# A recurrent-memory attention step on one core: one product for a maximum, one for each mask, a 64-wide turn of the memory, and a projection unit split in two

## The chip, the cores and the metric

The kernel runs on one core of one Trainium2 chip. The metric is the device time of one execution in microseconds (us). "Engine" below means one of the core's instruction streams: PE multiplies matrices (PEld is its weight loading, which overlaps it), DVE and ACT work on vectors, POOL is the general-purpose one, SP issues transfers.

## The reference

Four layers follow each other, A, B, A, B, each added to a residual of 2048 tokens by 640 channels. The change is in layer B, cut here to what matters:

```python
for s in range(n_seg):                       # 64 segments of 32 tokens
    xs = x[:, s * 32:(s + 1) * 32, :]
    h = concatenate([mem, xs], axis=1)       # 8 memory rows + 32 tokens = 40 rows
    q, k, v = h @ Wq, h @ Wk, h @ Wv         # 32 heads of 128, each from 640 channels
    scores = q @ k.T * scale                 # 40 x 40 for each head
    scores = where(mask, scores, -1e9)
    p = softmax(scores)
    o = (p @ v) @ Wo                         # back to 640 channels
    mem = o[:, :8, :]                        # memory of the next segment
    outs.append(o[:, 8:, :])
```

Segment s + 1 needs the memory that segment s made, so the 64 segments of a layer run one after the other, in two layers: 128 steps.

## The kernel before, in words

`layer_B` holds one loop over the 64 steps. The instructions of PE, ACT, DVE and POOL run in exactly the order in which the code issues them (`_OrdNC` chains each engine's instructions), so the order of the lines is the order on each engine.

The 32 tokens and 8 memory rows of a step are held so that 32 rows (24 tokens and the memory, `b_HX`) go through the step itself, and the other 8 tokens of each segment (the "tail" rows) go through projections for four steps at a time (`b_TX`). Most products have a stationary operand of only 32 columns. Four of them are placed side by side in PE's array, at columns 0, 32, 64 and 96 (`tile_position=(0, 32 * j)`), and run at the same time. The profile writes such a product's weights as 128*32. The products of probabilities with values use 32 (or 8) rows and all 128 columns instead (32*128, 8*128), and the turns of normalised tokens use the whole array (128*128).

One step goes as follows. The names are those of the tiles in the profile.

1. K and Q of heads 0 to 15, then of heads 16 to 31 (`b_Ka`, `b_Qa`, `b_Kb`, and Q's second half as `b_Qb` and `b_Qc`), each five groups of four products. ACT copies each out of PSUM and DVE transposes it (`turn`) into `b_KT` and `b_QT`.
2. For each half of the heads, a (b = 0) and b (b = 1): `mask_mm` writes the mask into a PSUM tile `b_SP` by products of an identity with `b_mask5`, and `scores` adds 32 small products per half. Groups of V of half a (`b_Va`) stand between them.
3. The softmax of each half: `soft_max` (DVE, negated maximum), `soft_sub` (DVE adds it to the scores), `soft_exp` (ACT), `soft_sum` and `soft_rec` (DVE), `soft_p` (POOL multiplies), `p_turn` (two DVE transposes into `b_PTa` or `b_PTb`).
4. Meanwhile PE does V of half b (`b_Vb`, five groups), one chunk of a deferred output projection (`od_chunk(0)`, tile `b_OPSd`), one tail unit (`tail_unit`, tile `b_tail`: five groups that project the tail rows of a later group of four steps), and in some steps `ln_spread` (five whole-array turns, `b_lntps`; 15 blocks of 128 tokens and 3 blocks of tail rows per layer are spread inside the loop). ACT copies the tail unit out (`b_tu`).
5. `pv(0)` and `pv(1)`: probabilities times values of the halves (`b_OTP`), copied by DVE and ACT into `b_OTsb`. DVE turns the tail unit (`tail_turn`).
6. Two groups of a small unit of V of tail rows (`b_vtail`, five groups in all), the output projection (`b_OPS`, 64 products), `od_chunk(1)`, a `b_vtail` group. In one step of four, and three more per layer, DVE begins a layer norm here (`ln_begin`).
7. The memory: ACT copies `b_OPS` in three parts into `b_msb`; for each part PE turns it by small products with `b_sel` (`b_MT`), followed by a group of `b_vtail` after the first and second part, and DVE copies the result into the next step's `b_HX`. The next `b_Ka` waits for that.

The PSUM tiles of steps 1 to 7 come in rotation from five buffers, and `b_tail` (shared with `b_Qc`), the tile of `b_OPS` (shared with `b_lntps`) and `b_OPSd` have one each.

Of the kernel before, what the change touches and what calls it, by code (L numbers as in the profile page):

```python
# [18 lines left out]
F32 = mybir.dt.float32  # L19
BF16 = mybir.dt.bfloat16  # L20
ACT = mybir.ActivationFunctionType
ALU = mybir.AluOpType
AX = mybir.AxisListType
# [6 lines left out]
NCH = 5  # L30
# [776 lines left out]
def layer_B(nc, tc, C, W, x_src, xb_src, x_dst, mem0, B_Wv, B_Wo, nsteps=64, out_bf16=False, tag=""):  # L807
    SCB = 1.0 / math.sqrt(128.0)
    nc_raw = nc
    nc = _OrdNC(tc, nc_raw, engines=ORDER_ENGINES)  # L810
# [3 lines left out]
    with ExitStack() as ctx:  # L814
# [16 lines left out]
        wkl = pool("b_wkl", 1)  # L831
        wk = pool("b_wk", 1)
        sm = pool("b_sm", 2)
# [5 lines left out]
        po = psum("b_po", 1)  # L839

        def ps_tile(shape, dtype, name):
            return pp.tile(shape, dtype, name=name, tag="ps")
# [3 lines left out]
        mask5, selm = C.mask5, C.selm  # L846
# [14 lines left out]
        def evac(eng, dst, src, scale=None):  # L861
            if eng == "act":
                if scale is None:
                    nc.scalar.copy(dst, src)
                else:
                    nc.scalar.activation(out=dst, in_=src, func=ACT.Copy, scale=scale)
            else:
                if scale is None:
                    nc.vector.tensor_copy(dst, src)
                else:  # L870
                    nc.vector.tensor_scalar(out=dst, in0=src, scalar1=scale, scalar2=None, op0=ALU.mult)
# [40 lines left out]
        def cols_of(u):  # L912
            return HX[u // 4][:, :, u % 4, :]

        def thin_mm(cols_ap, Wt, b, name, c0=0, c1=NCH, ps=None):
            if ps is None:
                ps = ps_tile([128, 512], F32, name)
            for c in range(c0, c1):
                for j in range(4):
                    n = 4 * b + j  # L920
                    nc.tensor.matmul(ps[32 * j:32 * j + 32, :], lhsT=cols_ap[:, c, :], rhs=Wt[:, c, 512 * n:512 * n + 512],
                                     start=(c == 0), stop=(c == NCH - 1), tile_position=(0, 32 * j), skip_group_check=True)
            return ps

        def by_head(cols_ap, Wt, h0, nh, ps):
            for c in range(NCH):
                wt = Wt[:, c, 128 * h0:128 * (h0 + nh)].rearrange("p (h e) -> p h e", e=128)
                for j in range(4):
                    nc.tensor.matmul(ps[32 * j:32 * j + 32, :].rearrange("p (h x) -> p h x", x=32), lhsT=cols_ap[:, c, :], rhs=wt[:, :, 32 * j:32 * j + 32],
                                     start=(c == 0), stop=(c == NCH - 1), tile_position=(0, 32 * j), skip_group_check=True)  # L930
            return ps
# [16 lines left out]
        def tail_cols(g, c=None):  # L948
            v = TX[g // 4][:, :, 4 * (g % 4):4 * (g % 4) + 4, :].rearrange("p c s t -> p c (s t)")
            return v if c is None else v[:, c]  # L950

        def tail_unit(g, k, ps):
            proj, b = divmod(k, 2)
            return by_head(tail_cols(g), W.wq if proj else W.wk, 16 * b, 16, ps)

        def tail_evac(k, ps):
            sb = kqp.tile([128, 512], BF16, name="b_tu", tag="kq")
            evac("act", sb[:], ps[:], SCB if k // 2 else None)
            return sb
# [47 lines left out]
        for k in WO_FIRST + WO_LAST:  # L1007
            f = load_B_wo(nc, W, B_Wo, k)
# [7 lines left out]
        tsb = []  # L1016
        for k in range(4):
            ps = tail_unit(0, k, ps_tile([128, 512], F32, "b_tail"))
# [13 lines left out]
        for k in range(4):  # L1032
            ps = vtail_unit(0, k)
# [56 lines left out]
        for s in range(nsteps):  # L1090
            last = (s == nsteps - 1)
            u = s + 1
            cols = cols_of(s)
            unit = (s // 4 + 1, s % 4) if s // 4 + 1 < NG else None
            work = unit or (None if last else (NG - 1, 0))
# [13 lines left out]

            def mask_mm(b):  # L1110
                SP = ps_tile([128, 5, 40], F32, f"b_SP{b}")
                for j in range(4):
                    nc.tensor.matmul(SP[32 * j:32 * j + 32].rearrange("p g k -> p (g k)"), lhsT=C.identb[:, 32 * j:32 * j + 32], rhs=mask5[:].rearrange("p g k -> p (g k)"),
                                     start=True, stop=False, tile_position=(0, 32 * j), skip_group_check=True)
                return SP

            def scores(b, SP):
# [6 lines left out]
                            nc.tensor.matmul(SP[32 * j:32 * j + 32, 0 if tail else 1 + i, :], lhsT=lhsT, rhs=KT[s][:, h, :],  # L1124
                                             start=False, stop=True, tile_position=(0, 32 * j), skip_group_check=True)

            negmax = sm.tile([128, 2, 5], F32, name="b_negmax", tag="negmax")
            ssum = sm.tile([128, 2, 5], F32, name="b_ssum", tag="ssum")
            rs = sm.tile([128, 2, 5], F32, name="b_rs", tag="rs")
            E_ = wk.tile([128, 2, 5, 40], BF16, name="b_E", tag="E0")  # L1130

            def soft_max(b, SP):
                nc.vector.tensor_reduce(out=negmax[:, b, :], in_=SP[:], axis=AX.X, op=ALU.max, negate=True)

            def soft_sub(b, SP):
                nc.vector.tensor_tensor(out=SP[:], in0=SP[:], in1=negmax[:, b, :].unsqueeze(2).to_broadcast([128, 5, 40]), op=ALU.add)

            def soft_exp(b, SP):
                nc.scalar.activation(out=E_[:, b], in_=SP[:], func=ACT.Exp)

            def soft_sum(b):
                nc.vector.tensor_reduce(out=ssum[:, b, :], in_=E_[:, b], axis=AX.X, op=ALU.add)

            def soft_rec(b):
                nc.vector.reciprocal(out=rs[:, b, :], in_=ssum[:, b, :])

            def soft_p(eng, b):
                eng.tensor_tensor(out=Pn[:, b, :, 0:40], in0=E_[:, b], in1=rs[:, b, :].unsqueeze(2).to_broadcast([128, 5, 40]), op=ALU.mult)

            def p_turn(b, PT):  # L1150
                nc.vector.transpose(out=PT[:, :, :, 8:40], in_=Pn[:, b, 1:5, :].rearrange("p g (a k) -> p a g k", a=2))
                nc.vector.transpose(out=PT[:, :, :, 0:8], in_=Pn[:, b, 0, :].rearrange("p (a i t) -> p a i t", a=2, i=4))
# [20 lines left out]
            for b in range(2):  # L1173
                for nm, Wt, D_, scale in (("K", W.wk, KT, None), ("Q", W.wq, QT, SCB)):
# [4 lines left out]
                    else:  # L1179
                        ps = by_head(cols, Wt, 16 * b, 16, ps_tile([128, 512], F32, f"b_{nm}{'ab'[b]}"))  # L1180
# [5 lines left out]
            SPb = mask_mm(1)  # L1186
            thin_mm(cols, W.wv, 0, "b_Va", 3, 4, Va)
            scores(1, SPb)
            thin_mm(cols, W.wv, 0, "b_Va", 4, NCH, Va)
            PTa = wkl.tile([128, 2, 4, 40], BF16, name="b_PTa", tag="PTa")  # L1190
            PTb = wkl.tile([128, 2, 4, 40], BF16, name="b_PTb", tag="PTb")
            soft_max(0, SPa)
            soft_sub(0, SPa)
            soft_exp(0, SPa)
            soft_max(1, SPb)
            soft_sub(1, SPb)
            soft_sum(0)
            soft_rec(0)
            soft_p(nc.gpsimd, 0)
            soft_exp(1, SPb)  # L1200
            evac("act", VH[s][:, 0, :], Va[:])
            soft_sum(1)
            soft_rec(1)
            soft_p(nc.gpsimd, 1)
            p_turn(0, PTa)
            p_turn(1, PTb)
            Vb = thin_mm(cols, W.wv, 1, "b_Vb")
            evac("act", VH[s][:, 1, :], Vb[:])
            if not last:
                od_chunk(0)  # L1210

            if work:
                tps = tail_unit(work[0], work[1], po.tile([128, 512], F32, name="b_tail", tag="tail"))
            if unit:
                tsb = tail_evac(unit[1], tps)
            if ln_ready:
                ln_spread(ln_ready.pop(0), po.tile([128, NCH, 4, 32], BF16, name="b_lntps", tag="ops"))
            if last:
# [9 lines left out]
            OTv = OTsb[:].rearrange("p (a x) -> p a x", a=2)  # L1228
            pv(0, PTa, ots)
            evac("dve", OTv[:, 0, 0:160], otf[0][:].rearrange("p i c -> p (i c)"))  # L1230
            ot01 = ps_tile([128, 4, 40], F32, "b_OTP1")
            ots[0][1] = ot01[:]
            pv(1, PTb, ots)
            evac("act", OTv[:, :, 160:320], otf[1][:].rearrange("p a i c -> p a (i c)"))
            evac("dve", OTv[:, 1, 0:160], ot01[:].rearrange("p i c -> p (i c)"))
            evac("act", OTv[:, :, 480:640], otf[3][:].rearrange("p a i c -> p a (i c)"))
            evac("dve", OTv[:, :, 320:480], otf[2][:].rearrange("p a i c -> p a (i c)"))
            if not last and (s + 1) % 4:
                vtails_in(s + 1)
# [17 lines left out]
            if not last:  # L1257
                dst = cols_of(s + 1)
                msb = wk.tile([128, 320], BF16, name="b_msb", tag="msb")
                parts = ((0, 1), (1, 3), (3, NCH))  # L1260
                for ca, cb in parts:
                    nc.scalar.copy(msb[:, 64 * ca:64 * cb], ops[:, 64 * ca:64 * cb])
                for pi, (ca, cb) in enumerate(parts):
                    mt = ps_tile([128, cb - ca, 8], F32, f"b_MT{pi}")
                    for c in range(ca, cb):
                        for q in range(4):
                            o = 64 * c + 32 * (q % 2)
                            nc.tensor.matmul(mt[32 * q:32 * q + 32, c - ca, :], lhsT=msb[:, o:o + 32], rhs=selm[:, q // 2, :],
                                             start=True, stop=True, tile_position=(0, 32 * q), skip_group_check=True)
                    nc.vector.tensor_copy(dst[:, ca:cb, 24:32], mt[:])  # L1270
                    vtail_some((1, 1, NCH)[pi])
            vtail_some(NCH)
# [114 lines left out]
```

## Time and profile before

| what | value |
|---|---|
| time, 3 runs | 2427.61, 2425.11, 2420.36 us; median 2425.11 |
| the profiled execution | 2418.85 us, its span 2417.1 us |
| granted clock of PE | 0.997 |
| PE busy | 2289.2 us (95%), 62330 products |
| DVE busy | 1882.4 us (78%) |
| ACT busy | 1416.2 us (59%) |
| POOL busy | 749.8 us (31%) |

The span runs from the first to the last instruction. The profiled execution's own time is 1.75 us more than its span. In the rows of the timeline the columns are: start in us from the span's start, duration in us (of all merged instructions together), engine, line, operation, what is written and read, count, and in brackets the idle time before it with what ended it. Most of layer B's rows have the line of one helper (L113), so they are told apart by tile.

### The profile page before, as it was taken

The numbers are of one execution on the slowest core, as the hardware profiler recorded it, in microseconds if no ns is written. First come the engines' busy times: TensorE is split into PE (matmuls) and PEld (weight loads), VectorE is DVE, ScalarE is ACT, GpSimd is POOL, SyncE is SP. The second block draws the span as 40 slices with busy tenths as digits, with TensorE's granted clock in tenths as the row PEclk, the third lists the DMA queues.
The fourth block names the chain that finished last, engine by engine and source line by source line (L and its number), as shares of the span: only waits on it lengthen the run. The fifth ranks groups of instructions, "written<-read, shape, count | busy, mean of one in ns | idle before, by whom it ended". The sixth has DMA issues, their size and how long they took to land.

```text
span 2417.1 us, 139330 instructions
## 1 busy us (share of the span) xinstructions
PE 2289.2 (95%) x62330; PEld 1504.1 (62%) x62330; DVE 1882.4 (78%) x4695; ACT 1416.2 (59%) x3198; POOL 749.8 (31%) x1589
## 2 busy tenths in 40 slices
PE   8999999999999999999989999999999999999998
PEld 5566656666666666666655665566666666666665
DVE  8999877777777777777679998777777777777776
ACT  6999964444444444444369999644444444445443
POOL 5677641111111111111146776411111111111111
PEclk9999999999999999999999999999999999999999
DMA  4121271111111111111220211711111111111110
GB/s 168 47 85 60 73 260 27 28 32 32 29 30 30 31 29 32 29 31 28 65 88 17 64 45 38 274 24 26 29 28 27 27 27 28 27 29 29 27 24 20
DMA packets 168883, 123.38 MB, mean 51 GB/s; under 512 B 104652, under 2 KB 153180, under 8 KB 166492
## 3 DMA queue, kind: packets, MB, share of 16 engines
q1 hardware_dynamic: 167288, 112.69, 16.4%
q8 instruction: 487, 7.98, 1.4%
q10 hardware_dynamic: 996, 1.79, 0.2%
q14 instruction: 112, 0.92, 0.1%
HBM read 79.60 MB, written 34.80 MB: 47 GB/s over the span
## 4 chain that ended last, share of the span: by engine, by line
PE 67%; DVE 14%; ACT 9%; DMA 4%; issue 3%; POOL 1%; SPq 1%; ACTq 0%; DVEq 0%; POOLq 0%
PE b_OPS L113 11%; PE b_Ka L113 6%; PE b_Kb L113 5%; PE b_Qa L113 5%; DVE a_nm L142 5%; PE b_tail L113 5%; PE b_Va L113 4%; PE b_Vb L113 4%; ACT a_PT L142 4%; PE b_vtail L113 4%; PE a_S L113 3%; PE b_SP L113 2%; PE b_OPSd L113 2%; PE b_OTP L113 2%; PE b_Qb L113 2%
## 5 line engine op out<-in xcount | busy, mean ns | idle before, releaser
L113 PEld LDWEIGHTS <-b_HX 128*32 128x32 bf16 x17920 | 467.0, 96 | 269.0 <-DVE b_HX L113 3.6
L113 POOL TENSOR_TENSOR b_Pn<-b_E,b_rs 128x200 bf16<-128x200 bf16 x256 | 133.4, 522 | 1092.7 <-DVE b_rs L113 1074.6
L142 DVE TENSOR_REDUCE a_nm<-a_S 128x2 f32<-128x512 f32 (+3 forms) x512 | 395.4, 817 | 52.8 <-PE a_S L113 37.5
L142 ACT ACTIVATE a_PT<-a_T 128x1024 bf16<-128x1024 f32 (+1 forms) x384 | 345.5, 905 | 22.8 <-PE a_T L113 15.0
L113 PE MATMUL b_OPS<-b_wo,b_OTsb 128*32 128x320 bf16 x8192 | 306.5, 300 | 4.6 <-DVE b_OTsb L113 3.6
L113 PEld LDWEIGHTS <-b_OTsb 128*32 128x32 bf16 x8192 | 208.1, 96 | 73.8 <-DVE b_OTsb L113 24.8
L113 DVE STREAM_TRANSPOSE b_KT<-b_kq 128x512 bf16<-128x512 bf16 x256 | 181.3, 708 | 80.3 <-ACT b_kq L113 79.7
L142 POOL TENSOR_SCALAR_AFFINE_SELECT a_PT<-a_PT 128x256 bf16<-128x256 bf16 x380 | 189.3, 503 | 152.5 <-ACT a_PT L142 151.0
L113 ACT ACTIVATE b_E<-b_SP 128x200 bf16<-128x200 f32 x256 | 86.3, 337 | 235.5 <-DVE b_SP L113 225.4
L113 PE MATMUL b_Va<-b_wv,b_HX 128*32 128x512 bf16 x2560 | 222.4, 381 | 0.0
L113 DVE CAST b_HX<-b_MT 128x16 bf16<-128x16 f32 (+1 forms) x380 | 64.7, 172 | 198.3 <-PE b_MT L113 190.0
L113 DVE STREAM_TRANSPOSE b_QT<-b_kq 128x256 bf16<-128x256 bf16 (+1 forms) x384 | 184.2, 505 | 39.3 <-ACT b_kq L113 35.9
L113 ACT CAST b_msb<-b_OPS 128x64 bf16<-128x64 f32 x378 | 69.3, 256 | 213.2 <-PE b_OPS L113 213.2
L113 PEld LDWEIGHTS <-b_TX 128*32 128x32 bf16 x5360 | 144.1, 96 | 58.4 <-issue 5.3
L113 DVE CAST b_OTsb<-b_OTP 128x160 bf16<-128x160 f32 (+1 forms) x384 | 133.8, 376 | 44.7 <-PE b_OTP L113 40.8
L113 PE MATMUL b_Ka<-b_wk,b_HX 128*32 128x512 bf16 x2560 | 163.5, 381 | 1.0 <-DVE b_HX L113 0.9
L113 PE MATMUL b_Vb<-b_wv,b_HX 128*32 128x512 bf16 x2560 | 162.2, 379 | 0.0
L113 PE MATMUL b_Qa<-b_wq,b_HX 128*32 128x512 bf16 x2560 | 161.1, 379 | 0.0
L113 PE MATMUL b_Kb<-b_wk,b_HX 128*32 128x512 bf16 x2560 | 161.1, 379 | 0.0
L113 PE MATMUL b_vtail<-b_wv,b_TX 128*32 128x256 bf16 x2680 | 149.7, 273 | 1.3 <-issue 0.7
L113 ACT CAST b_kq<-b_Ka 128x512 bf16<-128x512 f32 x128 | 74.9, 585 | 123.0 <-PE b_Ka L113 123.0
L113 ACT CAST b_OTsb<-b_OTP 128x320 bf16<-128x320 f32 x256 | 96.5, 429 | 81.4 <-PE b_OTP L113 81.0
(185 smaller groups left out, 5048.3 us busy)
## 6 DMA issues: line engine op xcount, KB each, us to landing
b_wv<-in_B_Wv_dram SPq DMA_DIRECT2D x10, 1024.0 KB
b_wo<-in_B_Wo_dram SPq DMA_DIRECT2D x16, 640.0 KB
b_VT<-b_VTd SPq DMA_DIRECT2D x504, 16.0 KB
b_XO<-xres SPq DMA_DIRECT2D x256, 30.0 KB
b_VTd<-b_vt SPq DMA_DIRECT2D x480, 16.0 KB
b_xt<-xres_bf SPq DMA_DIRECT2D x40, 160.0 KB
b_wk<-in_B_Wk_dram SPq DMA_DIRECT2D x20, 256.0 KB
b_wq<-in_B_Wq_dram SPq DMA_DIRECT2D x20, 256.0 KB
```

The lines of the kernel that those rows point to most:

```text
L113: r = f(*a, **k)
L142: r = f(*a, **k)
```

## The change

Five edits, all inside `layer_B`:

- The negated maximum of half b is made in BF16, and `soft_sub(1)` no longer is a DVE addition but one whole-array product of the identity with that maximum, repeated along the 40 columns, added to the scores in PSUM. It stands on PE after the third of the five groups of `b_Vb`; before the change all of `b_Vb` was issued in one piece. Half a keeps its DVE addition.
- Each mask is written by one whole-array product in place of four products of 32 columns.
- The memory is turned by products whose stationary operand is 64 columns wide: two for each 128 channels in place of four.
- The tail unit is split: three groups stand where it stood, two stand between `pv(0)` and `pv(1)`. Its copy by ACT (`b_tu`) moves behind both of ACT's copies into `b_OTsb`.
- Order of the softmax: `soft_exp(1)` is issued before `soft_sum(0)`; `p_turn(0)` ahead of POOL's second product.

```diff
--- before.py
+++ after.py
@@ -922,8 +922,8 @@
                                      start=(c == 0), stop=(c == NCH - 1), tile_position=(0, 32 * j), skip_group_check=True)
             return ps
 
-        def by_head(cols_ap, Wt, h0, nh, ps):
-            for c in range(NCH):
+        def by_head(cols_ap, Wt, h0, nh, ps, c0=0, c1=NCH):
+            for c in range(c0, c1):
                 wt = Wt[:, c, 128 * h0:128 * (h0 + nh)].rearrange("p (h e) -> p h e", e=128)
                 for j in range(4):
                     nc.tensor.matmul(ps[32 * j:32 * j + 32, :].rearrange("p (h x) -> p h x", x=32), lhsT=cols_ap[:, c, :], rhs=wt[:, :, 32 * j:32 * j + 32],
@@ -949,9 +949,9 @@
             v = TX[g // 4][:, :, 4 * (g % 4):4 * (g % 4) + 4, :].rearrange("p c s t -> p c (s t)")
             return v if c is None else v[:, c]
 
-        def tail_unit(g, k, ps):
+        def tail_unit(g, k, ps, c0=0, c1=NCH):
             proj, b = divmod(k, 2)
-            return by_head(tail_cols(g), W.wq if proj else W.wk, 16 * b, 16, ps)
+            return by_head(tail_cols(g), W.wq if proj else W.wk, 16 * b, 16, ps, c0, c1)
 
         def tail_evac(k, ps):
             sb = kqp.tile([128, 512], BF16, name="b_tu", tag="kq")
@@ -1109,9 +1109,8 @@
 
             def mask_mm(b):
                 SP = ps_tile([128, 5, 40], F32, f"b_SP{b}")
-                for j in range(4):
-                    nc.tensor.matmul(SP[32 * j:32 * j + 32].rearrange("p g k -> p (g k)"), lhsT=C.identb[:, 32 * j:32 * j + 32], rhs=mask5[:].rearrange("p g k -> p (g k)"),
-                                     start=True, stop=False, tile_position=(0, 32 * j), skip_group_check=True)
+                nc.tensor.matmul(SP[:].rearrange("p g k -> p (g k)"), lhsT=C.identb[:], rhs=mask5[:].rearrange("p g k -> p (g k)"),
+                                 start=True, stop=False, skip_group_check=True)
                 return SP
 
             def scores(b, SP):
@@ -1124,16 +1123,20 @@
                             nc.tensor.matmul(SP[32 * j:32 * j + 32, 0 if tail else 1 + i, :], lhsT=lhsT, rhs=KT[s][:, h, :],
                                              start=False, stop=True, tile_position=(0, 32 * j), skip_group_check=True)
 
-            negmax = sm.tile([128, 2, 5], F32, name="b_negmax", tag="negmax")
+            negmax = [sm.tile([128, 5], dt_, name=f"b_negmax{b}", tag=f"negmax{b}") for b, dt_ in enumerate((F32, BF16))]
             ssum = sm.tile([128, 2, 5], F32, name="b_ssum", tag="ssum")
             rs = sm.tile([128, 2, 5], F32, name="b_rs", tag="rs")
             E_ = wk.tile([128, 2, 5, 40], BF16, name="b_E", tag="E0")
 
             def soft_max(b, SP):
-                nc.vector.tensor_reduce(out=negmax[:, b, :], in_=SP[:], axis=AX.X, op=ALU.max, negate=True)
+                nc.vector.tensor_reduce(out=negmax[b][:], in_=SP[:], axis=AX.X, op=ALU.max, negate=True)
 
             def soft_sub(b, SP):
-                nc.vector.tensor_tensor(out=SP[:], in0=SP[:], in1=negmax[:, b, :].unsqueeze(2).to_broadcast([128, 5, 40]), op=ALU.add)
+                shift = negmax[b][:].unsqueeze(2).to_broadcast([128, 5, 40])
+                if b:
+                    nc.tensor.matmul(SP[:], lhsT=C.identb[:], rhs=shift, start=False, stop=True, skip_group_check=True)
+                else:
+                    nc.vector.tensor_tensor(out=SP[:], in0=SP[:], in1=shift, op=ALU.add)
 
             def soft_exp(b, SP):
                 nc.scalar.activation(out=E_[:, b], in_=SP[:], func=ACT.Exp)
@@ -1187,32 +1190,31 @@
             thin_mm(cols, W.wv, 0, "b_Va", 3, 4, Va)
             scores(1, SPb)
             thin_mm(cols, W.wv, 0, "b_Va", 4, NCH, Va)
-            PTa = wkl.tile([128, 2, 4, 40], BF16, name="b_PTa", tag="PTa")
-            PTb = wkl.tile([128, 2, 4, 40], BF16, name="b_PTb", tag="PTb")
             soft_max(0, SPa)
             soft_sub(0, SPa)
             soft_exp(0, SPa)
             soft_max(1, SPb)
+            Vb = thin_mm(cols, W.wv, 1, "b_Vb", 0, 3)
+            PTa = wkl.tile([128, 2, 4, 40], BF16, name="b_PTa", tag="PTa")
+            PTb = wkl.tile([128, 2, 4, 40], BF16, name="b_PTb", tag="PTb")
             soft_sub(1, SPb)
+            soft_exp(1, SPb)
+            thin_mm(cols, W.wv, 1, "b_Vb", 3, NCH, Vb)
             soft_sum(0)
             soft_rec(0)
             soft_p(nc.gpsimd, 0)
-            soft_exp(1, SPb)
             evac("act", VH[s][:, 0, :], Va[:])
             soft_sum(1)
             soft_rec(1)
+            p_turn(0, PTa)
             soft_p(nc.gpsimd, 1)
-            p_turn(0, PTa)
             p_turn(1, PTb)
-            Vb = thin_mm(cols, W.wv, 1, "b_Vb")
             evac("act", VH[s][:, 1, :], Vb[:])
             if not last:
                 od_chunk(0)
 
             if work:
-                tps = tail_unit(work[0], work[1], po.tile([128, 512], F32, name="b_tail", tag="tail"))
-            if unit:
-                tsb = tail_evac(unit[1], tps)
+                tps = tail_unit(work[0], work[1], po.tile([128, 512], F32, name="b_tail", tag="tail"), 0, 3)
             if ln_ready:
                 ln_spread(ln_ready.pop(0), po.tile([128, NCH, 4, 32], BF16, name="b_lntps", tag="ops"))
             if last:
@@ -1228,12 +1230,16 @@
             OTv = OTsb[:].rearrange("p (a x) -> p a x", a=2)
             pv(0, PTa, ots)
             evac("dve", OTv[:, 0, 0:160], otf[0][:].rearrange("p i c -> p (i c)"))
+            if work:
+                tail_unit(work[0], work[1], tps, 3, NCH)
             ot01 = ps_tile([128, 4, 40], F32, "b_OTP1")
             ots[0][1] = ot01[:]
             pv(1, PTb, ots)
             evac("act", OTv[:, :, 160:320], otf[1][:].rearrange("p a i c -> p a (i c)"))
             evac("dve", OTv[:, 1, 0:160], ot01[:].rearrange("p i c -> p (i c)"))
             evac("act", OTv[:, :, 480:640], otf[3][:].rearrange("p a i c -> p a (i c)"))
+            if unit:
+                tsb = tail_evac(unit[1], tps)
             evac("dve", OTv[:, :, 320:480], otf[2][:].rearrange("p a i c -> p a (i c)"))
             if not last and (s + 1) % 4:
                 vtails_in(s + 1)
@@ -1263,10 +1269,9 @@
                 for pi, (ca, cb) in enumerate(parts):
                     mt = ps_tile([128, cb - ca, 8], F32, f"b_MT{pi}")
                     for c in range(ca, cb):
-                        for q in range(4):
-                            o = 64 * c + 32 * (q % 2)
-                            nc.tensor.matmul(mt[32 * q:32 * q + 32, c - ca, :], lhsT=msb[:, o:o + 32], rhs=selm[:, q // 2, :],
-                                             start=True, stop=True, tile_position=(0, 32 * q), skip_group_check=True)
+                        for q in range(2):
+                            nc.tensor.matmul(mt[64 * q:64 * q + 64, c - ca, :], lhsT=msb[:, 64 * c:64 * c + 64], rhs=selm[:, q, :],
+                                             start=True, stop=True, tile_position=(0, 64 * q), skip_group_check=True)
                     nc.vector.tensor_copy(dst[:, ca:cb, 24:32], mt[:])
                     vtail_some((1, 1, NCH)[pi])
             vtail_some(NCH)
```

## The prediction

> **What bounds the kernel now.** I read the page first (busy shares, then the chain that ended last), then the busy time of one plain step, then that step's timeline engine by engine.
>
> ```profile
> PE 2289.2 (95%) x62330; PEld 1504.1 (62%) x62330; DVE 1882.4 (78%) x4695; ACT 1416.2 (59%) x3198; POOL 749.8 (31%) x1589
> ...
> PE 67%; DVE 14%; ACT 9%; DMA 4%; issue 3%; POOL 1%; SPq 1%; ACTq 0%; DVEq 0%; POOLq 0%
> ...
> L113 ACT CAST b_msb<-b_OPS 128x64 bf16<-128x64 f32 x378 | 69.3, 256 | 213.2 <-PE b_OPS L113 213.2
> ```
>
> PE is busy 95% and carries two thirds of the chain. The memory's copies come three to a step, so 378 / 3 = 126 steps turn a memory; the code runs 128 steps, and the last of each layer turns none. One step without `b_lntps`:
>
> ```profile
> 763.74:776.92 13.18, 12.75 (x428) 8.42 (x416) 9.30 (x27) 6.35 (x16) 2.12 (x5) 1.00 0.09 19
> ```
>
> The columns are length, then busy us of PE, PEld, DVE, ACT, POOL, then the granted clock (full). PE is busy for 12.75 of 13.18 us; DVE has 3.9 us to spare. So what DVE loses counts only where DVE stands on the step's chain, and what PE gains in time counts nearly everywhere.
>
> ```profile
> 768.08 0.26 PE L113 MATMUL b_SP<-b_mask,c_identb 128*32 128x200 bf16 x4
> 768.16 0.39 PE L113 MATMUL b_Va<-b_wv,b_HX 128*32 128x512 bf16 x4
> ...
> 769.79 1.27 PE L113 MATMUL b_Vb<-b_wv,b_HX 128*32 128x512 bf16 x20
> ...
> 770.87 0.46 PE L113 MATMUL b_OPSd<-b_wo,b_OTdef 128*32 128x320 bf16 x8
> ...
> 771.14 1.27 PE L113 MATMUL b_tail<-b_wq,b_TX 128*32 128x512 bf16 x20
> ```
>
> Starts tell PE's pace (ends are modelled). Five groups of `b_Vb` take 770.87 - 769.79 = 1.08 us, 0.216 a group; the chunk of `b_OPSd` 0.27. Four mask products of 200 columns take 768.16 - 768.08 = 0.08, which is 200/512 of a group: side by side, they already cost what one product of 200 columns would.
>
> ```profile
> 769.96 0.36 DVE L113 TENSOR_REDUCE b_negmax<-b_SP 128x5 f32<-128x200 f32 x1
> 770.17 0.34 ACT L113 ACTIVATE b_E<-b_SP 128x200 bf16<-128x200 f32 x1 [1.49 <-DVE b_SP L113]
> 770.36 0.37 DVE L113 TENSOR_TENSOR b_SP<-b_SP,b_negmax 128x200 f32<-128x200 f32 x1
> 770.64 0.35 DVE L113 TENSOR_REDUCE b_ssum<-b_E 128x5 f32<-128x200 bf16 x1
> 770.82 0.34 ACT L113 ACTIVATE b_E<-b_SP 128x200 bf16<-128x200 f32 x1 [0.31 <-DVE b_SP L113]
> ...
> 771.02 0.19 DVE L113 RECIPROCAL b_rs<-b_ssum 128x5 f32<-128x5 f32 x1
> ...
> 771.19 0.36 DVE L113 TENSOR_REDUCE b_ssum<-b_E 128x5 f32<-128x200 bf16 x1
> 771.36 1.11 POOL L113 TENSOR_TENSOR b_Pn<-b_E,b_rs 128x200 bf16<-128x200 bf16 x2 [9.57 <-DVE b_rs L113]
> ...
> 771.59 0.19 DVE L113 RECIPROCAL b_rs<-b_ssum 128x5 f32<-128x5 f32 x1
> 771.91 0.57 DVE L113 STREAM_TRANSPOSE b_PTa<-b_Pn 128x256 bf16<-128x256 bf16 x2
> 772.50 0.57 DVE L113 STREAM_TRANSPOSE b_PTb<-b_Pn 128x256 bf16<-128x256 bf16 x2
> 772.51 0.60 ACT L113 ACTIVATE b_tu<-b_tail 128x512 bf16<-128x512 f32 x1 [0.38 <-PE b_tail L113]
> 772.54 0.20 PE L113 MATMUL b_OTP<-b_PTa,b_Vth 32*128 32x40 bf16 x4
> ...
> 773.22 0.20 PE L113 MATMUL b_OTP<-b_PTb,b_Vth 32*128 32x40 bf16 x4 [0.30 <-ACT b_tu L113]
> ```
>
> This is the softmax that PE waits for. `pv(0)` starts at 772.54, 0.06 after `b_PTa` ends (771.91 + 0.57); `pv(1)` at 773.22, 0.15 after `b_PTb` ends (772.50 + 0.57). The bracket names `b_tu`, whose end at 773.11 nearly coincides; I take `b_PTb`, because `pv(1)` reads it. PE's idle time lies here.
>
> **The price of a change of shape.** Three edits put products of another width between groups of 128*32. The trace shows what that costs where it happens already:
>
> ```profile
> 931.87 1.27 PE L113 MATMUL b_tail<-b_wq,b_TX 128*32 128x512 bf16 x20
> 933.06 0.28 PEld L113 LDWEIGHTS <-b_xt 128*128 128x128 bf16 x5 [0.42 <-issue]
> 933.07 0.45 PE L113 MATMUL b_lntps<-c_identb,b_xt 128*128 128x128 bf16 x5
> 933.45 0.20 PE L113 MATMUL b_OTP<-b_PTa,b_Vth 32*128 32x40 bf16 x4
> ...
> 773.40 0.20 PE L113 MATMUL b_OTP<-b_PTb,b_VT 8*128 8x40 bf16 x4
> 773.53 0.40 PE L113 MATMUL b_vtail<-b_wv,b_TX 128*32 128x256 bf16 x8
> ```
>
> Five tail groups from 931.87 end at 932.95; the turn starts at 933.07: 0.12 lost, and its weight load waited 0.42 for nothing that the profile shows. Five turns of 128 columns (128/512 of a group, 0.28 for all) end at 933.35; `pv` starts at 933.45: 0.10. The last `pv` products (40 columns, 0.02) end at 773.42; the next group starts at 773.53: 0.11. I take 0.10 per change, with 0.12 as the upper end. For 64-wide products no row exists; the bounds are zero (as between equal shapes, mask to `b_Va`) and 0.12, and I take 0.10, since every change of shape that the trace does show costs it.
>
> The Trainium skill says so too (TensorEngine Tiling (Array Packing), Key Properties): changing the tiling mode, not just the tile, drains the engine; it lists 128×64 as a mode of its own. By that rule the 64-wide turns pay as well, and the sum would be the one below. The trace agrees for 128*128 and 32*128; no run here shows 64.
>
> **Part by part, in the plain step.** *Masks.* Each product lasts 0.08 as before, and changes shape twice: +0.20 each, +0.40 for both. PE runs gapless through this stretch, so `b_Vb` starts 0.40 late.
>
> *The product for the maximum.* The third `b_Vb` group would end at 769.79 + 0.65 = 770.44; with five changes of shape the product starts at 770.94. Half b's maximum is done by then: before it ended at 770.32, and even a full 0.40 late it ends at 770.72, so PE doesn't wait for it. Such a product runs some 0.25 (mask row), and a consumer follows 0.05 later, as `b_HX` does after `b_MT` below. `soft_exp(1)` starts at 771.24 instead of 770.82: +0.42. The DVE addition that went (0.37) gives half a 0.09 in `soft_sum(0)`, which then waits for the exponential alone (end 770.51).
>
> *Softmax to `pv(1)`.* Half b's sum and reciprocal move with its exponential, the reciprocal to 772.01-772.20. They stand ahead of `p_turn(0)` on DVE, so `b_PTa` can't start before 772.20 and ends at 772.77 (+0.29). POOL's second product starts 0.15 after the reciprocal, as its first does (771.21 to 771.36), at 772.35, and ends at 772.90 (half of 1.11); `b_PTb` 772.93 to 773.50; `pv(1)` 773.65 by this path.
>
> *The tail unit on both sides.* On PE: product 770.94 + 0.08 + 0.10 = 771.12, two `b_Vb` groups 0.43, `b_OPSd` 0.27, three tail groups 0.65: 772.47. Then PE waits for `b_PTa` and starts `pv(0)` at 772.83. It lasts 0.20 (as 773.22 to 773.42), a change 0.10, two tail groups 0.43, a change 0.10: `pv(1)` at 773.66. So both paths end together and `pv(1)` is 0.44 late; the split fills a wait with work, and its two changes hide in it. Without that wait they would cost 0.20. In steps with `b_lntps`, PE arrives last: 772.47 + 0.10 + 0.28 + 0.10 = 772.95, `pv(1)` at 773.78, 0.12 more. The code spreads 18 blocks per layer inside the loop: 36 such steps.
>
> *`b_tu` moved.*
>
> ```profile
> 773.76 0.75 ACT L113 CAST b_OTsb<-b_OTP 128x320 bf16<-128x320 f32 x2 [0.66 <-PE b_OTP L113]
> ...
> 774.31 0.70 DVE L113 STREAM_TRANSPOSE b_tQ<-b_tu 128x512 bf16<-128x512 bf16 x1
> ```
>
> It now follows both copies: 774.51 + 0.44 = 774.95, 0.60 long, its transpose at about 775.6 to 776.3. What DVE does next is due for `b_HX` at 776.70 + 0.44, so plain steps hide it. Where a layer norm stands between, its statistics can push that copy by some tenths, but PE is late there too (next part): 0 to 0.1 in 36 steps, at most 4 us; I take 0.
>
> *The memory 64 wide.*
>
> ```profile
> 776.24 0.28 PE L113 MATMUL b_vtail<-b_wv,b_TX 128*32 128x256 bf16 x4
> 776.46 0.19 PE L113 MATMUL b_MT<-b_sel,b_msb 128*32 128x8 bf16 x4
> 776.50 0.28 PE L113 MATMUL b_vtail<-b_wv,b_TX 128*32 128x256 bf16 x4
> 776.62 0.21 PE L113 MATMUL b_MT<-b_sel,b_msb 128*32 128x8 bf16 x8
> 776.69 0.28 PE L113 MATMUL b_vtail<-b_wv,b_TX 128*32 128x256 bf16 x4
> 776.70 0.59 DVE L113 CAST b_HX<-b_MT 128x8 bf16<-128x8 f32 x3 [1.68 <-PE b_MT L113]
> 776.80 0.21 PE L113 MATMUL b_MT<-b_sel,b_msb 128*32 128x8 bf16 x8
> 776.92 1.26 PE L113 MATMUL b_Ka<-b_wk,b_HX 128*32 128x512 bf16 x20
> ```
>
> Eight turns take 776.69 - 776.62 = 0.07, so four save 0.035 twice. But `b_vtail` groups stand between, so there are six changes. The first hides: the group from 776.24 and a change end at 776.45. From 776.46: 0.01 turn, 0.10, 0.11 group, 0.10, 0.035, 0.10, 0.11, 0.10, 0.035, 0.10: `b_Ka` after 0.80 instead of 0.46, +0.34. With changes free it would be 0.30, and `b_HX` would hold `b_Ka` where it is.
>
> **Sum.** Per step 0.44 + 0.34 = 0.78; 126 x 0.78 = 98.3; 36 x 0.12 = 4.3; the two last steps about 1. In all 103.6 on the profiled execution's 2418.85: 2522. The runs' median stands 6.3 above that execution (2425.11), which would give 2529. I forecast 2525, slower by 4%.
>
> **Rivals.** *Changes of shape cost nothing here, and it is faster.* For it: a product of the identity needs no data that is late, so its weights could be loaded ahead, as those of equal shape are. Against it: the wait of 0.42 before `b_xt`, whose data was long there. Then `soft_exp(1)` starts at 770.44 + 0.30 = 770.74, `soft_sum(0)` at 770.55, POOL at 771.27 and 771.82, `b_PTa` ends at 772.42, `b_PTb` at 772.99, `pv(1)` at 773.14: 0.08 earlier, 126 x 0.08 = 10 us, 2409. It decides below about 0.016 us a change, where five changes eat the 0.08. Chance 0.06.
>
> The Trainium skill has a rule for that (TensorE: Matmul & The Clock Gate, Part 2): PE may pull a weight load ahead of running products where the row groups don't conflict or it goes to the background buffer. By it the result would be that 2409. The trace shows it for equal shapes only, and against it for `b_xt`.
>
> *The 64-wide turns are no change of shape.* For it: the same 128 rows. Against: all shown changes cost the same, whatever rows or columns differ. Then 126 x 0.44 + 4.3 + 1 = 61: 2480. Chance 0.10.
>
> *DVE becomes the bound.* If the 64-wide turns are free, the late `b_tu` comes to bear in the 36 steps with a layer norm; that adds up to 0.4 x 36 = 14 to the 2480. Chance 0.04.
>
> **How the numbers follow.** The forecast has 0.80. Its own range: with 0.12 a change, `pv(1)` comes 0.14 later (five changes before the exponential and two around the tail groups) and the memory 0.10, 126 x 0.24 = 30 more: up to 2552; with a tenth less per part down to 2500. The range 2475 to 2552 takes in the 64-wide rival. A measurement of this kernel can tell 0.3% (7 us) from no change. Faster: the first rival, 0.06. Same: 0.02, if changes cost about the 0.016 that breaks even. Slower: 0.92.
>
> **What would show it.** Right: in the changed profile `b_Va` starts about 0.28 after the mask product and the mask about 0.10 later than Qc's pace allows; the product for the maximum is preceded by PE waiting for nothing shown; `soft_exp(1)` 0.4 later; `b_PTa` right behind the second reciprocal; from the first `b_MT` to `b_Ka` 0.8; a step of about 13.96. Wrong: 128*128 or 64-wide products that start at the pace of their neighbours, a `b_MT` stretch still at 0.46, or PE waiting for the maximum.

## The result, and the profile after

The changed kernel takes 2540.81 us (median of 4 runs, 2536.60 to 2544.46); the kernel before, run beside it, 2426.36 us. The ratio is 1.0479 (95% interval 1.0453 to 1.0506): slower by 4.8%, inside the range, 16 us above the forecast. The page of the changed kernel, its busy shares and its chain that ended last:

```profile
PE 2452.5 (96%) x60430; PEld 1462.3 (58%) x60430; DVE 1840.1 (72%) x4567; ACT 1409.5 (55%) x3198; POOL 751.6 (30%) x1589
...
PE 80%; DVE 8%; ACT 8%; issue 2%; DMA 1%; POOL 0%; SPq 0%; ACTq 0%; DVEq 0%; POOLq 0%
```

PE issues 1900 fewer products and is busy 163 us longer. DVE has 42 us less work, but what counts is the chain: PE's part of it grew from 67% to 80%, and DVE's fell from 14% to 8%. The time lies in the steps, here a plain one and one with `b_lntps` (length, then busy us of PE, PEld, DVE, ACT, POOL, as before):

```profile
808.99:823.09 14.10, 14.05 (x405) 8.16 (x401) 9.86 (x27) 6.25 (x17) 2.13 (x5) 1.00 0.14 32
894.33:908.63 14.30, 14.30 (x410) 8.35 (x406) 9.53 (x26) 6.82 (x18) 3.58 (x9) 1.00 0.14 32
```

Before, they were 13.18 and 13.19. The plain step grew by 0.92, and 126 x 0.92 = 116 us accounts for the result (114.5 us between the medians). Added up over all 126 steps of the two traces, the steps grew by 117 us, from 1682.9 to 1800.0; the two profiled executions as a whole are 125.6 us apart. The timeline of the plain step, with `b_Ka` at 808.99 (763.74 before):

```profile
813.44 0.26 PE L113 MATMUL b_SP<-b_mask,c_identb 128*128 128x200 bf16 x1
...
813.63 0.40 PE L113 MATMUL b_Va<-b_wv,b_HX 128*32 128x512 bf16 x4
...
814.08 0.63 PE L113 MATMUL b_Va<-b_wv,b_HX 128*32 128x512 bf16 x8
...
814.64 0.26 PE L113 MATMUL b_SP<-b_mask,c_identb 128*128 128x200 bf16 x1
814.83 0.40 PE L113 MATMUL b_Va<-b_wv,b_HX 128*32 128x512 bf16 x4
...
815.50 0.84 PE L113 MATMUL b_Vb<-b_wv,b_HX 128*32 128x512 bf16 x12
815.55 0.37 DVE L113 TENSOR_REDUCE b_negmax<-b_SP 128x5 bf16<-128x200 f32 x1 [0.20 <-PE b_SP L113]
...
816.27 0.10 PEld L113 LDWEIGHTS <-c_identb 128*128 128x128 bf16 x1 [0.42 <-issue]
816.27 0.26 PE L113 MATMUL b_SP<-b_negmax,c_identb 128*128 128x200 bf16 x1
816.46 0.61 PE L113 MATMUL b_Vb<-b_wv,b_HX 128*32 128x512 bf16 x8
...
816.57 0.34 ACT L113 ACTIVATE b_E<-b_SP 128x200 bf16<-128x200 f32 x1 [0.77 <-PE b_SP L113]
816.69 0.32 PEld L113 LDWEIGHTS <-b_OTdef 128*32 128x32 bf16 x8
...
816.90 0.44 PE L113 MATMUL b_OPSd<-b_wo,b_OTdef 128*32 128x320 bf16 x8
...
817.33 0.19 DVE L113 RECIPROCAL b_rs<-b_ssum 128x5 f32<-128x5 f32 x1
817.44 0.53 DVE L113 STREAM_TRANSPOSE b_PTa<-b_Pn 128x256 bf16<-128x256 bf16 x2
817.69 0.52 POOL L113 TENSOR_TENSOR b_Pn<-b_E,b_rs 128x200 bf16<-128x200 bf16 x1 [0.60 <-DVE b_rs L113]
818.03 0.20 PE L113 MATMUL b_OTP<-b_PTa,b_Vth 32*128 32x40 bf16 x4
...
818.25 0.57 DVE L113 STREAM_TRANSPOSE b_PTb<-b_Pn 128x256 bf16<-128x256 bf16 x2 [0.28 <-POOL b_Pn L113]
...
818.33 0.61 PE L113 MATMUL b_tail<-b_wk,b_TX 128*32 128x512 bf16 x8
...
818.97 0.20 PE L113 MATMUL b_OTP<-b_PTb,b_Vth 32*128 32x40 bf16 x4
...
820.79 0.71 DVE L113 STREAM_TRANSPOSE b_tK<-b_tu 128x512 bf16<-128x512 bf16 x1 [0.64 <-ACT b_tu L113]
```

Between the start of a mask product and that of the next `b_Va` lie 0.19 us, where the work is 0.08: 0.11 for the change back. Two `b_Va` groups from 814.08 end at 814.51, by the pace of 0.216 a group; the mask starts at 814.64: 0.13 for the change there. The third `b_Vb` group ends at 816.15, the product for the maximum starts at 816.27: 0.12; the maximum was ready at 815.92, so PE didn't wait for it. The weight loads show the change as well: those of this product start only with it, after 0.42 in which their loader waited for nothing that the profile shows, while those of `b_OPSd`, whose products have the shape of the groups before them, start at 816.69, 0.21 ahead. DVE now waits for PE ahead of the maximum (0.20), where it waited for nothing before. The second exponential starts 7.58 into the step instead of 7.08, `pv(1)` 9.98 instead of 9.48: 0.50 late. The memory's stretch:

```profile
822.21 0.20 PE L113 MATMUL b_MT<-b_sel,b_msb 128*64 128x8 bf16 x2
822.33 0.29 PE L113 MATMUL b_vtail<-b_wv,b_TX 128*32 128x256 bf16 x4
...
822.55 0.23 PE L113 MATMUL b_MT<-b_sel,b_msb 128*64 128x8 bf16 x4
822.71 0.29 PE L113 MATMUL b_vtail<-b_wv,b_TX 128*32 128x256 bf16 x4
...
822.93 0.23 PE L113 MATMUL b_MT<-b_sel,b_msb 128*64 128x8 bf16 x4
...
823.09 0.83 PE L113 MATMUL b_Ka<-b_wk,b_HX 128*32 128x512 bf16 x12
```

A `b_vtail` group needs 0.11 (256/512 of 0.216), but 0.22 pass from each to the next turn; from four turns to the next group it is 0.16, where from eight it was 0.07. From the first turn to `b_Ka`: 0.88 instead of 0.46. So the step grew by 0.50 ahead of `pv(1)` and 0.42 at the memory.

### The profile page after: what moved, and what is told of

Its sections match the earlier page's. It is cut to its first block, busy times and chain, and to the rows that moved or that the text cites. A ratio compares the mean times of both kernels' runs of the same rounds, so it can differ in the third digit from the quotient of the medians.

```text
span 2542.7 us, 135152 instructions
## 1 busy us (share of the span) xinstructions
PE 2452.5 (96%) x60430; PEld 1462.3 (58%) x60430; DVE 1840.1 (72%) x4567; ACT 1409.5 (55%) x3198; POOL 751.6 (30%) x1589
## 4 chain that ended last, share of the span: by engine, by line
PE 80%; DVE 8%; ACT 8%; issue 2%; DMA 1%; POOL 0%; SPq 0%; ACTq 0%; DVEq 0%; POOLq 0%
PE b_OPS L113 11%; PE b_Va L113 7%; PE b_tail L113 6%; PE b_Ka L113 6%; PE b_Vb L113 6%; PE b_Kb L113 5%; PE b_Qa L113 5%; PE b_SP L113 5%; PE b_vtail L113 5%; ACT a_PT L142 4%; DVE a_nm L142 4%; PE b_OTP L113 4%; PE b_Qb L113 3%; PE b_Qc L113 3%; PE b_OPSd L113 3%; PE a_S L113 3%
## 5 line engine op out<-in xcount | busy, mean ns | idle before, releaser
L113 PEld LDWEIGHTS <-b_HX 128*32 128x32 bf16 x17920 | 442.3, 96 | 272.6
L113 PE MATMUL b_Va<-b_wv,b_HX 128*32 128x512 bf16 x2560 | 235.4, 385 | 0.0
L113 PEld LDWEIGHTS <-c_identb 128*128 128x128 bf16 x1312 | 107.7, 98 | 176.1 <-issue 152.1
L113 PE MATMUL b_Vb<-b_wv,b_HX 128*32 128x512 bf16 x2560 | 185.8, 381 | 0.0
L113 PE MATMUL b_vtail<-b_wv,b_TX 128*32 128x256 bf16 x2680 | 166.9, 279 | 0.9 <-issue 0.7
```

The source lines that it names most:

```text
L113: r = f(*a, **k)
```

## The experiments

Theory: every change of shape on PE, into a product of another shape and out of it, costs about 0.11 us, wherever PE has no wait that hides it. Rivals: the place of the product for the maximum and the order on DVE; the whole-array and 64-wide products slow by themselves; a split tail unit that costs nothing. Each ratio is to the kernel before, run alongside, with its 95% interval; differences between ratios are turned into us with 2424. The edits are shown shortened.

**Undoing one shape at a time**, each from the changed kernel.

```diff
 # masks_four
-nc.tensor.matmul(SP, lhsT=C.identb[:], rhs=mask5, ...)
+for j in range(4): nc.tensor.matmul(SP[32*j:32*j+32], lhsT=C.identb[:, 32*j:32*j+32], rhs=mask5, tile_position=(0, 32*j), ...)
```

> The changed kernel with each mask written by four products of 32 columns again; all else as changed. Theory (each change of shape on PE costs about 0.10 to 0.12 us where PE has no wait): Vb starts 0.45 us earlier in the step, the product for the maximum and the second exponential too; PTa then ends 0.28 earlier, held by POOL's first product, and pv(1) comes 0.40 earlier, held by PE's two tail groups. 128 x 0.40 = 51, so about 2489 us. Rival (the product for the maximum is late because of its place behind three Vb groups and of the order on DVE, whatever the masks' shape): within 10 us of 2541.

2492.81 us, 1.0284 (1.0268 to 1.0299): 1.0479 - 1.0284 = 1.95%, 47 us back of the 51 expected. The rival falls.

```diff
 # turn_32
-for q in range(2): nc.tensor.matmul(mt[64*q:64*q+64], lhsT=msb[:, 64*c:64*c+64], rhs=selm[:, q], tile_position=(0, 64*q))
+for q in range(4): nc.tensor.matmul(mt[32*q:32*q+32], lhsT=msb[:, o:o+32], rhs=selm[:, q // 2], tile_position=(0, 32*q))
```

> The changed kernel with the memory turned by four products of 32 columns for each 128 channels again; all else as changed. Theory: from the first MT product to Ka 0.47 us again instead of 0.89, so 126 x 0.42 = 53 less; steps with a layer norm give back up to 0.16 each because DVE's statistics, pushed by the later tail transpose, now come before the copy that Ka waits for (36 x 0.16 = 6): 2488 to 2494 us. Rival (the memory's stretch is bound by ACT's copies or by DVE, and 64-wide products are only as slow as the wait): within 10 us of 2541.

2491.46 us, 1.0279 (1.0264 to 1.0295): 2.00%, 49 us back, within the 47 to 53 that the theory had.

```diff
 # max_four
-nc.tensor.matmul(SP[:], lhsT=C.identb[:], rhs=shift, ...)
+for j in range(4): nc.tensor.matmul(SP[32*j:32*j+32], lhsT=C.identb[:, 32*j:32*j+32], rhs=shift, tile_position=(0, 32*j), ...)
```

> The changed kernel with the product for half b's maximum done as four products of 32 columns side by side, at the same place; masks and memory as changed. Theory: two changes of shape go, one of them ahead of the second exponential, so pv(1) comes 0.12 us earlier: 128 x 0.12 = 15, and some 3 in steps with lntps: about 2523 us. Rival (place and order, not shape): 2541 us, no difference.

2518.39 us, 1.0388 (1.0373 to 1.0404): 0.91%, 22 us back, where 18 were expected. Place and order are the same, so they aren't what made it late.

**The same products, fewer changes.** These two keep every whole-array and 64-wide product and only move what stands between them.

```diff
 # masks_adjacent
 SPa = mask_mm(0)
+SPb = mask_mm(1)
 Va = thin_mm(...)
 ...
-SPb = mask_mm(1)
```

> The changed kernel with one line moved: the whole-array mask of half b is issued right behind that of half a, so the two need two changes of shape instead of four; the same products. Theory: Vb, the product for the maximum and the second exponential come 0.22 us earlier, pv(1) as well: 128 x 0.22 = 28, about 2513 us. Rival (the whole-array product itself is slow, its weights of 128 columns or its writes): 2541 us, no difference.

2511.22 us, 1.0344 (1.0326 to 1.0362): 1.35%, 33 us back, where 28 were expected. In its timeline the two masks and the next group:

```profile
844.53 0.34 PE L113 MATMUL b_SP<-b_mask,c_identb 128*128 128x200 bf16 x2
...
844.80 0.40 PE L113 MATMUL b_Va<-b_wv,b_HX 128*32 128x512 bf16 x4
```

Two products take 0.27 up to the next group: 2 x 0.08 for the work and 0.11 for one change. The second mask costs only its work.

```diff
 # turn_64_grouped: all vtail groups left follow the last turn
 nc.vector.tensor_copy(dst[:, ca:cb, 24:32], mt[:])
-vtail_some((1, 1, NCH)[pi])
```

> The changed kernel with the vtail groups that stand between the 64-wide turns issued behind the last turn: the same products, two changes of shape around the turns instead of six. Theory: the turns then wait for ACT's copies (0.17 us apart), the last ends 0.39 after the first, one change and two groups follow, and Ka starts 0.71 after the first turn instead of 0.89: 126 x 0.18 = 22 less, about 2519 us, although PE now waits twice for ACT with nothing beside it. Rival (the 64-wide products or their weight loads are slow themselves): 2541 us or more, since the waits come on top.

2515.75 us, 1.0362 (1.0346 to 1.0378): 1.17%, 28 us back, where 22 were expected.

```profile
857.93 0.57 PE L113 MATMUL b_MT<-b_sel,b_msb 128*64 128x8 bf16 x10
...
858.43 0.40 PE L113 MATMUL b_vtail<-b_wv,b_TX 128*32 128x256 bf16 x8
858.65 0.61 PE L113 MATMUL b_Ka<-b_wk,b_HX 128*32 128x512 bf16 x8
```

`b_Ka` follows the first turn by 0.72 instead of 0.88, although PE now waits for ACT's copies with nothing beside them. So the price is that of the change of shape, for 64-wide products too; the rival that the products are slow explains at most the 0.05 that the second pair of four turns takes.

**What is left without the shapes.**

all_thin is the changed kernel with the three edits above together.

> The changed kernel with masks, memory and the product for the maximum all made of 32-column products; what stays is the maximum taken off on PE, the order of the softmax and the tail unit on both sides of pv(0). Theory: the exponential comes 0.08 us earlier than in the kernel before, but PE's two tail groups with a change of shape before and after them hold pv(1) 0.08 later than before (126 x 0.08 = 10), and steps with a layer norm lose up to 0.16 (6): 2430 to 2443 us against 2426. Rival (the shapes are a minor part): 2480 us or more.

2439.77 us, 1.0068 (1.0051 to 1.0085), inside what was expected: the three shapes make 4.1 of the 4.8%. Alone they gave back 47 + 49 + 22 = 118 us, together 100: when the exponential comes early again, the split tail unit holds `pv(1)` instead, as the next two runs show.

```diff
 # all_thin_tail_whole, from all_thin
-tps = tail_unit(..., 0, 3)
+tps = tail_unit(...)
+if unit: tsb = tail_evac(unit[1], tps)
 ...
-if work: tail_unit(work[0], work[1], tps, 3, NCH)      # between pv(0) and pv(1)
 ...
-if unit: tsb = tail_evac(unit[1], tps)                 # behind ACT's copies into b_OTsb
```

> The kernel with all products 32 columns wide (as all_thin) and the tail unit in one piece at its old place, its copy too. What is left of the change is half b's maximum taken off on PE and the order of the softmax. Theory: without the two changes of shape between pv(0) and pv(1), pv(1) follows PTb, 0.06 to 0.08 us a step earlier than in the kernel before: 128 x 0.07 = 9, so 2413 to 2419 us against 2424, the fastest of all. Rival (the split itself is harmless, and the 16 us of all_thin come from the maximum on PE): 2435 to 2440 us.

2421.37 us, 0.9993 (0.9979 to 1.0007): no difference from before, not the 9 us hoped for; but 18 us faster than all_thin, so the split is what all_thin lost. Its profiled execution took 2434.21 us, so only lengths that many of its steps have are read from it. The plain step (`b_Ka` at 782.62, the next at 795.73), a step with `b_lntps`, and the `b_Vb` of such a step before (its `pv(0)` is the row at 933.45 above):

```profile
789.32 0.28 PE L113 MATMUL b_SP<-b_negmax,c_identb 128*32 128x200 bf16 x4
...
789.63 0.34 ACT L113 ACTIVATE b_E<-b_SP 128x200 bf16<-128x200 f32 x1 [0.24 <-PE b_SP L113]
...
792.03 0.20 PE L113 MATMUL b_OTP<-b_PTb,b_Vth 32*128 32x40 bf16 x4 [0.31 <-DVE b_PTb L113]
```

```profile
814.91 0.84 PE L113 MATMUL b_Vb<-b_wv,b_HX 128*32 128x512 bf16 x12
...
817.93 0.20 PE L113 MATMUL b_OTP<-b_PTa,b_Vth 32*128 32x40 bf16 x4
...
818.39 0.33 DVE L113 CAST b_OTsb<-b_OTP 128x160 bf16<-128x160 f32 x1 [0.27 <-PE b_OTP L113]
...
818.77 0.40 PE L113 MATMUL b_vtail<-b_wv,b_TX 128*32 128x256 bf16 x8
```

```profile
930.52 1.27 PE L113 MATMUL b_Vb<-b_wv,b_HX 128*32 128x512 bf16 x20
```

The exponential at 7.01 and `pv(1)` at 9.41 are the 0.07 that were expected, and the plain step takes 13.11 instead of 13.18. But in steps with `b_lntps` PE works without a gap from `b_Vb` to `pv(0)`, here and before, so the product for the maximum comes on top: 3.02 from `b_Vb` to `pv(0)` (814.91 to 817.93) instead of 2.93 (930.52 to 933.45). DVE's copy of `pv(0)` ends at 818.72, and `b_vtail` waits for that copy's PSUM tile: this step runs from 808.85 to 822.14, 13.29; the most frequent length of such steps is 13.26, and before it was 13.19. So 90 x 0.07 - 36 x 0.07 to 0.10 = 3 to 4 us less is left, inside the interval.

```diff
 # tail_split_alone, from the kernel before: the inverse of the edit above
```

> The kernel before with one edit: the tail unit split on both sides of pv(0), its copy moved as in the change. Theory: PE goes pv(0), change, two groups, change, pv(1), so pv(1) comes 0.14 us later a step (126 x 0.14 = 17), plus up to 6 in steps with a layer norm: 2438 to 2447 us against 2424. Rival (the split fills a wait and costs nothing): 2424 us.

2452.99 us, 1.0112 (1.0099 to 1.0125): +27 us, more than the 14 to 23 expected.

```profile
836.30 0.57 DVE L113 STREAM_TRANSPOSE b_PTb<-b_Pn 128x256 bf16<-128x256 bf16 x2
836.34 0.20 PE L113 MATMUL b_OTP<-b_PTa,b_Vth 32*128 32x40 bf16 x4 [0.57 <-DVE b_PTa L113]
...
836.65 0.61 PE L113 MATMUL b_tail<-b_wq,b_TX 128*32 128x512 bf16 x8
...
837.20 0.20 PE L113 MATMUL b_OTP<-b_PTb,b_Vth 32*128 32x40 bf16 x4
```

`b_PTb` is ready at 836.87, but PE is in its two groups: from `pv(0)` to `pv(1)` 0.86 instead of 0.68. That is 0.18 x 126 = 22. The rest is the layer norm's statistics (`b_ln_st`), which stand behind the tail unit's transpose on DVE and come later with it. A step with them:

```profile
866.39 0.84 DVE L113 BATCH_NORM_STATS2 b_ln_st<-b_xt 128x6 f32<-128x320 bf16 x2
...
867.51 0.21 PE L113 MATMUL b_MT<-b_sel,b_msb 128*32 128x8 bf16 x8
867.59 0.42 DVE L113 CAST b_HX<-b_MT 128x8 bf16<-128x8 f32 x3
```

DVE comes to the copies that the next `b_Ka` waits for only after the last turns have started; in the plain step before, it started the first of them ahead of these (776.70 and 776.80). In this trace the 36 steps with `b_ln_st` last 13.53 in the median and the other 90 last 13.37: 0.16 x 36 = 6, the most that was expected, and 28 us in all.

**One shape alone.** max_one_alone is all_thin_tail_whole with the one whole-array product for the maximum.

> The changed kernel with masks and memory 32 columns wide and the tail unit whole at its old place; the maximum of half b is taken off by one whole-array product. Theory: its first change of shape (0.12) uses up what the DVE addition gave back (0.08), so the second exponential comes 0.04 us later than before and pv(1) with it: 128 x 0.04 = 5, 2424 to 2431 us against 2424; the second change of shape is hidden by the wait ahead of pv(0). Rival (the product on PE is a cost in itself, or a gain in itself): 2440 us or more, or 2415 or less.

2430.28 us, 1.0025 (1.0014 to 1.0035): +6 us, as expected. On its own the move of the subtraction to PE costs almost nothing and gains nothing. masks_one_alone is the kernel before with the change's mask product.

> The kernel before with one edit: each mask by one whole-array product. Theory: four changes of shape and no wait on PE to hide them make the scores of half b 0.45 us late; DVE takes its maximum 0.33 later, and everything behind it on DVE, the sum of half a too, so pv(1) comes 0.34 later: 128 x 0.34 = 44, about 2467 us against 2424. Rival (DVE, not PE, sets the softmax's pace, and the masks hide): 2424 to 2435 us.

2473.39 us, 1.0202 (1.0187 to 1.0216): +49 us, where 44 were expected. DVE's row shows the link that the theory named:

```profile
851.48 0.37 DVE L113 TENSOR_REDUCE b_negmax<-b_SP 128x5 f32<-128x200 f32 x1 [0.23 <-PE b_SP L113]
```

**A try for a faster one.** thin_ln_between is all_thin_tail_whole with `ln_spread` moved behind `pv(0)`.

> A try for a faster kernel: all products 32 columns wide, the tail unit whole at its old place, half b's maximum taken off on PE, and the turn of normalised tokens (lntps, in 36 steps) moved between pv(0) and pv(1), where PE waits for PTb. Theory: plain steps take 13.11 us instead of 13.19 as in all_thin_tail_whole, and steps with lntps no longer push pv(0) and with it the copy that vtail waits for, so they take about 13.15: 126 x 0.07 = 9 less than before, 2414 to 2418 us against 2424. Rival (what the steps with lntps lose is made elsewhere): 2421 us or more.

2430.41 us, 1.0014 (1.0002 to 1.0026): the rival's side. Plain steps take 13.11 again, but the most frequent lengths with `b_lntps` are 13.25 and 13.26, not 13.15. One of these:

```profile
725.46 0.69 ACT L113 COPY b_TX<-b_lntps 128x640 bf16<-128x640 bf16 x1
...
725.66 0.40 PE L113 MATMUL b_vtail<-b_wv,b_TX 128*32 128x256 bf16 x8
...
726.20 2.36 PE L113 MATMUL b_OPS<-b_wo,b_OTsb 128*32 128x320 bf16 x64
```

`pv(0)` is no longer pushed, but `b_OPS` shares its one PSUM tile with `b_lntps`, and ACT now empties that tile later. The copy ends at 726.15 and `b_OPS` starts at 726.20, though PE is through with its two `b_vtail` groups at 725.88; in all 36 steps `b_OPS` starts 0.05 or 0.06 after that copy ends. Why some of these steps last over 14 us, which none of them did before, stays open. No version beats the kernel before by more than a measurement can tell.

## Why the prediction was right, point by point

The direction, the mechanism and the stages held; the sizes were low, 0.78 us for the plain step instead of 0.92. In brackets stands what was forecast.

- *Masks:* `b_Vb` started 6.51 into the step instead of 6.05, 0.46 late (0.40). The term that was mis-sized is the price of a change: 0.10 was taken; the rows of after show 0.11 back and 0.12 to 0.13 in, at the upper end given or just above.
- *The product for the maximum* waited for nothing, as forecast; the exponential is 0.50 late (0.42).
- *Softmax:* `b_PTa` ended 0.24 late (0.29): its transpose starts at 817.44, 0.08 before the reciprocal ends. `pv(1)` is 0.50 late (0.44), held by `b_PTb` (818.82) alone and not by both paths together: PE's two tail groups end at 818.76, and with a change PE would have been free at 818.87, 0.10 before it went on. That the split's changes hide here stands, and tail_split_alone shows what they cost without the cover.
- *Steps with `b_lntps`:* the step above took 0.20 more than the plain one, but that overstates the growth: over all 36 the median rose from 13.26 to 14.30 and that of the others from 13.19 to 14.10, so they grew by 0.13 more (0.12).
- *Memory:* 0.42 (0.34): five changes at 0.11 to 0.12, and four 64-wide turns that take 0.05, not 0.035.
- *`b_tu`:* its transpose ran from 820.79 to 821.50, before the memory's copies needed DVE. The 36 steps with a layer norm have the median of the plain ones, 14.10, so the 0 taken for them was right.

By terms: 0.92 x 126 = 116 instead of 0.78 x 126 = 98. The first rival, free changes, has its own answer: without the changes of shape (all_thin_tail_whole) the plain step is 0.07 shorter, where 0.08 was said; but its 10 us overlooked the steps with `b_lntps`, and no gain can be told. The second rival, 64-wide products as no change of shape, falls by turn_32 and turn_64_grouped. The third, DVE as the bound, needed free 64-wide turns and falls with it. By the Trainium skill (TensorEngine Tiling (Array Packing), Key Properties), changing the tiling mode drains the engine. The trace now agrees for 64 columns as well: the `b_vtail` group from 822.33 ends at 822.44 by its pace, and the turn starts at 822.55, 0.11 later. Whether a change's 0.11 is the engine running empty, or the weight load that no longer runs ahead, no run here separates.

## What to carry to other kernels

Count products by their changes of shape, not by their number: four narrow products side by side that cost what one wide one does (0.08 us here) are cheaper, if the wide one makes the engine change shape on both sides (0.11 to 0.13 each). Put products of an odd shape together, or beside a wait that hides the change. Work that is split to fill a wait must fit into it with its changes, or it becomes the wait.

## What was not expected of the hardware

A change from 32 to 64 columns, with the same 128 rows, costs the same 0.11 us as one between rows and columns; the prediction had no row for it and took 0.10 by analogy. And 64-wide turns pair up worse than 32-wide ones: four of 64 columns take 0.05 (0.16 to the next group less 0.11), eight of 32 columns took 0.07, so half as many products save hardly any time.
